# One tails product for two batches, loads reordered behind a DMA transpose, and query/key tails placed by GpSimd, in a fused attention and MLP-Mixer kernel

## The chip, the cores and the metric

The kernel runs on one core of a Trainium2 chip. Its time is the device time of one execution in microseconds (us), the median of several runs; lower is better. The core's engines are TensorE (PE in the profile, with its weight loads as PEld), VectorE (DVE), ScalarE (ACT), GpSimd (POOL) and SyncE (SP, which issues most of the DMAs). Each engine works through its own queue in order.

## The reference

```
q, k, v: [8, 8, 576, 64] float32          # batch, heads, sequence, head size
scores = q @ k^T / 8
  heads 0-3: only keys with 0 <= i - j < 32
  heads 4-7: only keys with 0 <= i - j < 128 and (i - j) % 4 == 0
x = softmax(scores) @ v                    # [8, 576, 512], heads side by side
h = relu(x^T @ w_tok1) @ w_tok2            # over the sequence: 576 -> 256 -> 576
u = x + h^T
out = u + relu(u @ w_ch1) @ w_ch2          # over the channels: 512 -> 1536 -> 512
```

## The kernel before

All matrix work is in float16 with float32 sums. The sequence of 576 is split into a main part of 512 (4 blocks of 128) and a tail of 64. The eight batches go through a software pipeline. Stage `b` of the program is the channel part of batch `b` (`gen_main(b)`): twelve products `gp` of 128 channels x 512 positions (L645), each followed by a relu into `gta` on ACT or DVE (L648); the tails product `gt` (L636); and then the second channel product `yp` (L664, in two halves for each of four blocks), to which DVE adds `u` (L674) before the result goes out. An odd batch has one more block, s = 4 (L684), that does the tails of two batches at once: the tails of the even batch lie in rows 0 to 63 of `u16t`, those of the odd one in rows 64 to 127, and their hidden values in columns 512 to 575 and 576 to 639 of `gta`.

The tails product is made batch by batch: `gp_tails` runs after channel blocks 5 and 8, each time for six channel blocks of 64 columns in one PSUM bank, four matmuls (one for each 128 channels of u) for each block: 24 matmuls of 64 columns.

Between the pieces of `gen_main(b)` come steps of other batches, which `interleave` places by a planner's clock: each piece of the main generator and each step has a cost in us, a step is emitted as soon as the clock has reached its due time, and what is left when the main generator ends is emitted at once. In a stage b from 2 on these steps are, with their due times:

- for batch b+1: the attention's value products (`values`), the token part (`emit_h1`, `emit_u`) and the turning of u (`uT_dma`, `uT_place`). For batches from 3 on, u is turned by a transposing DMA on SP's queue (`utt` for the tails, L570; `utm` for the main part, L572), and `uT_place` has ACT put two of the four blocks into natural order (`utd`, L582). For batches 0 to 2, `emit_uT` turns u by TensorE transposes and copies.
- for batch b+2: casts of q, k and v to float16 on GpSimd (`cast_steps`), transposing DMAs of q and k on SP (`dma_steps`, L349), placement of the turned q and k (`place_steps`), and the scores (`score_steps`). `plain` (pairs 0 and 1: three GpSimd copies each, L371 and L373), `tails` (L367, L368) and `dil` and `dil_k` (L377, L382) write the places that the score matmuls read. A pair's scores are three steps: `sc` for each of its two heads (L406) and `sm` for the parts at the end of the sequence, which reads the tails. ACT's exp follows, and for batches from 2 on GpSimd multiplies by the masks (L113).
- for batch b+3: fourteen load DMAs of q, k and v on SP's queue (`load_steps`).

Stages 0 and 1 have due times of their own. In stage 0 the scores of batch 1 and the first two pairs of batch 2 are made, in stage 1 the other two pairs of batch 2 and all of batch 3, the first batch whose q and k come by DMA.

Of the kernel before, what the change touches and what calls it, by code (L numbers as in the profile page):

```python
# [16 lines left out]
S = 576  # L17
# [52 lines left out]
def kernel(  # L70
# [16 lines left out]
    def fixed(name, shape, dtype=FP16):  # L87
        return sb.tile(shape, dtype, tag=name, bufs=1, name=name)
# [10 lines left out]
    def copy(eng, out, in_):  # L99
        if eng is nc.scalar:  # L100
            nc.scalar.copy(out=out, in_=in_)  # L101
        else:
            eng.tensor_copy(out=out, in_=in_)  # L103
# [48 lines left out]
    w4 = [w4a[:, i] for i in range(NMB)]  # L152
    idle = fixed("idle", [128, 512])
    uTm = [fixed(f"utm{i}", [128, 4, 4, 128]) for i in range(2)]
    uTt = [fixed(f"utt{i}", [128, 4, 128]) for i in range(2)]
    uTd = fixed("utd", [128, 2, 512])

    def emit_fixed():
# [202 lines left out]
    def place_steps(b):  # L361

        halves = [slice(0, 64), slice(64, 128)]

        def tails():
            for h in range(2):
                nc.vector.tensor_copy(out=qza[halves[h], :, h, 512:S], in_=tta[halves[h], :, 0:64])  # L367
            nc.vector.tensor_copy(out=kta[:, :, 512:S], in_=tta[:, :, 64:128])  # L368

        def plain(hp):  # L370
            nc.gpsimd.tensor_copy(out=natural(kt[hp][:, 0:512]), in_=kra[:, hp].rearrange("p r m -> p m r"))  # L371
            for h in range(2):
                nc.gpsimd.tensor_copy(out=natural(qz[hp][halves[h], h, 0:512]),  # L373
                                      in_=qta[halves[h], hp].rearrange("p r m -> p m r"))

        def dil(h):
            nc.vector.tensor_copy(out=qza[halves[h], 2:4, h, 0:512],  # L377
                                  in_=qta[halves[h], 2:4].rearrange("p a r m -> p a (r m)"))

        def dil_k():  # L380
            for hp in (2, 3):
                nc.vector.tensor_copy(out=natural(kt[hp][:, 384:512]),  # L382
                                      in_=kra[:, hp, :, 96:128].rearrange("p r m -> p m r"))

        return ([lambda hp=hp: plain(hp) for hp in range(2)],
                [tails] + [lambda h=h: dil(h) for h in range(2)] + [dil_k])

    def first_tails():

# [151 lines left out]
    def emit_uT(b, cb):  # L541
        odd = b % 2
        p = bank("fl" if b or cb % 2 == 0 else "main", 3, f"tpu_{b}_{cb}", FP16)
        tl = u16t[b // 2][:, cb]
        t = sb.tile([128, S], FP16, tag="ut", bufs=5, name=f"uT_{b}_{cb}")
        eng = nc.scalar if cb == 2 or (b and cb == 3) else nc.vector
        if cb < 2:
            m0, t0, c0 = (128, 0, 64) if odd else (0, 512, 0)
            for s in range(4):
                nc.tensor.transpose(out=p[:, m0 + 128 * s:m0 + 128 * s + 128],  # L550
                                    in_=u16(b, s)[:, cb], identity=ident)
            nc.tensor.transpose(out=p[:, t0:t0 + 128], in_=tl, identity=ident)
            copy(eng, t, p[:, c0:c0 + S])
        else:
            grid = p[:, 0:4 * RS].rearrange("p (r i) -> p r i", i=RS)
            m0, t0, c0 = (32, 0, 16) if odd else (0, 128, 0)
            for s in range(4):
                nc.tensor.transpose(out=grid[:, s, m0:m0 + 128], in_=u16(b, s)[:, cb], identity=ident)
            nc.tensor.transpose(out=grid[:, :, t0:t0 + 32], in_=tl, identity=perm)
            copy(eng, natural(t), grid[:, :, c0:c0 + MR].rearrange("p r m -> p m r"))  # L560
        uT[(b, cb)] = (t[:, 64:S], t[:, 0:64]) if odd else (t[:, 0:512], t[:, 512:S])


    def turned(b):
        return b >= 3
# [1 line left out]
    def uT_dma(b, tail):  # L567
        i = b % 2
        if tail:
            nc.sync.dma_start_transpose(out=uTt[i], in_=u16t[b // 2].rearrange("p x c -> p (x c)"))  # L570
        else:
            nc.sync.dma_start_transpose(out=uTm[i].rearrange("p x s t -> p (x s) t"),  # L572
                                        in_=u16w[b].rearrange("p x s c -> p (x s c)"))

    def uT_place(b, cb):
        i = b % 2
        tail = uTt[i][:, cb, 64 * i:64 * i + 64]
        if cb < 2:
            uT[(b, cb)] = (uTm[i][:, cb].rearrange("p s t -> p (s t)"), tail)
        else:  # L580
            uT[(b, cb)] = (uTd[:, cb - 2], tail)
            nc.scalar.copy(out=natural(uTd[:, cb - 2]), in_=uTm[i][:, cb].rearrange("p r m -> p m r"))  # L582
# [23 lines left out]
    def mix_steps(b, t_h1, t_h1b, t_u, t_uT, du=1.0):  # L606
        h1 = [sb.tile([128, DM], FP16, tag="h1", bufs=4, name=f"h1_{b}_{jb}") for jb in range(2)]
        steps = []
        for half, at in ((0, t_h1), (1, t_h1b)):
            for jb in range(2):  # L610
                steps.append((at + 0.9 * jb, 0.55, lambda jb=jb, half=half: emit_h1(b, jb, half, h1[jb])))
        for i, s in enumerate((4, 0, 1, 2, 3)):
            steps.append((t_u + du * i, 0.44, lambda s=s: emit_u(b, s, h1)))
        if turned(b):
            for t, tail in ((2.0, True), (6.0, False)):
                steps.append((t_u + t * du, 0.0, lambda tail=tail: uT_dma(b, tail)))
            for i, cb in enumerate(CBS):
                steps.append((t_uT + 0.5 * i, 0.0, lambda cb=cb: uT_place(b, cb)))
        else:
            for i, cb in enumerate(CBS):  # L620
                steps.append((t_uT + 0.9 * i, 0.28, lambda cb=cb: emit_uT(b, cb)))
        return steps

    def gen_main(b):
        odd = b % 2
        order = CBS if b else range(4)
        m0, t0 = (640, 576) if odd else (0, 512)

        def w3_block(cb, mb):
            return w3[cb][:, 512 * (mb // 4) + mb % 4:512 * (mb // 4) + 512:4]  # L630

        def gp_tails(half):
            p = bank("main", 3, f"gt_{b}_{half}")
            for i in range(6):
                for cb in order:
                    nc.tensor.matmul(  # L636
                        out=p[:, 64 * i:64 * i + 64], lhsT=w3_block(cb, 6 * half + i), rhs=uT[(b, cb)][1],
                        start=(cb == order[0]), stop=(cb == order[-1]))
            relu(nc.scalar if half else nc.vector, gta[:, 6 * half:6 * half + 6, t0:t0 + 64],
                 p[:, 0:384].rearrange("p (i t) -> p i t", t=64))  # L640

        for mb in range(NMB):
            p = bank("main", 3, f"gp_{b}_{mb}")
            for i, cb in enumerate(order):
                nc.tensor.matmul(out=p, lhsT=w3_block(cb, mb), rhs=uT[(b, cb)][0], start=(i == 0), stop=(i == 3))  # L645
                if i == 1:
                    yield 0.43
            relu(nc.vector if mb % (2 if b == 0 else 4) == 1 else nc.scalar, gta[:, mb, m0:m0 + 512], p)  # L648
            yield 0.43
            if mb in (5, 8):  # L650
                gp_tails(int(mb == 8))
                yield 0.7
        last = b == B - 1
        for s in ((4, 0, 1, 2, 3) if odd else (0, 1, 2, 3)):
            p = bank("main", 3, f"yp_{b}_{s}")
# [105 lines left out]
    for jb in range(2):  # L761
        nc.gpsimd.tensor_copy(
            out=w2p[jb], in_=w2[jb][:, 0:512].rearrange("p (m r) -> p r m", r=4))
    for i in range(2):
        nc.gpsimd.memset(u16t[i][64:128], 0.0)

    warm(8)
    ts = [st[2] for st in score_steps(0, 0.0, 1.0)]
# [109 lines left out]
    for b in range(B):  # L878
# [15 lines left out]
        elif b == 1:  # L894
            late = score_steps(2, -4.3, 2.4, (0.0, 0.7, 1.6))
            va = value_steps(2, 4.2, 1.0)
            steps += late[10:] + va[:4] + [(9.6 + (0.0, 0.8, 2.8, 3.6)[i], c, f) for i, (_, c, f) in enumerate(va[4:])]
            steps += mix_steps(2, 10.8, 14.6, 17.2, 22.2)
            steps += score_steps(3, 22.2, 2.8) + at(9.0, 0.6, cast_steps(3))
            steps += at(6.0, 0.0, [lambda: load_v(3)]) + at(20.0, 0.9, load_steps(4))  # L900
            steps += at(15.0, 0.7, dma_steps(3)) + at(20.6, 0.4, place_steps(3)[0])
            steps += [(t, 0.0, f) for t, f in zip((21.6, 27.0, 27.8, 28.6), place_steps(3)[1])]
        else:
            if b + 1 < B:
                steps += value_steps(b + 1, 0.4, 0.95) + mix_steps(b + 1, 5.4, 9.0, 11.4, 29.2)
            if b + 2 < B:
                steps += at(2.0, 0.6, cast_steps(b + 2)) + score_steps(b + 2, 16.2, 2.7)
                steps += at(8.5, 0.7, dma_steps(b + 2)) + at(13.0, 0.4, place_steps(b + 2)[0])
                steps += [(t, 0.0, f) for t, f in zip((15.5, 19.2, 20.0, 20.8), place_steps(b + 2)[1])]
            if b + 3 < B:  # L910
                steps += at(13.0, 0.9, load_steps(b + 3))
        interleave(gen_main(b), steps)


# [28 lines left out]
```

## Time and profile before

| what | us |
|---|---|
| median of 3 runs | 298.76 (298.59 to 299.44) |
| time of the profiled execution | 298.87 |
| its span, first to last instruction | 297.1 |
| PE busy | 283.5 (95%) |
| POOL busy | 181.6 (61%) |
| DVE busy | 155.6 (52%) |
| ACT busy | 132.1 (44%) |

The granted TensorE clock is 1.000. In the trace a line of a timeline gives the start in us, the duration, engine, source line, operation, output and inputs, shape and count, and in brackets the idle time before it with what ended it. A matmul's duration is its whole way through the array; matmuls follow each other much closer, so distances between starts are what counts. A row of the windows view gives for each engine the busy time in that stretch.

Stages begin at about 28.9 us (0), 70.7 (1), 107.9 (2), 140.1 (3), 174.1 (4) and 205.4 (5).

### The profile page before, as it was taken

The page shows a single profiled execution, that of the slowest core. Times are in us where ns is not written, and L with a number is a line of the kernel's source. Part 1 is how long each engine was busy: PE and PEld are TensorE (multiplying, and loading weights), DVE is VectorE, ACT ScalarE, POOL GpSimd, SP SyncE. Part 2 cuts the span into 40 slices and gives each one's busy share as a digit, 9 for nine tenths or more (in the row PEclk, how much of TensorE's full clock was granted, in tenths as well). Part 3 has the DMA queues.
Part 4 walks back from the last instruction along what each step waited for, and adds up shares of the span by engine and source line. Part 5 has one row for each costly group of instructions (what it writes and reads, how often), then busy time and mean ns, then how long its engine had stood idle before and what let it go on. Part 6 is the DMA issues. An engine that isn't in the chain of part 4 may idle for free.

```text
span 297.1 us, 7477 instructions
## 1 busy us (share of the span) xinstructions
PE 283.5 (95%) x3012; PEld 221.4 (75%) x3012; DVE 155.6 (52%) x328; ACT 132.1 (44%) x258; POOL 181.6 (61%) x245
## 2 busy tenths in 40 slices
PE   5698999999999999999999999999999999999994
PEld 2596579986767987688676977697777977796594
DVE  5776338656837966632745155723843265423022
ACT  2763326456652634347444544356345624323400
POOL 7992056428998899839992999459992920000000
PEclk9999999999999999999999999999999999999999
DMA  7999999953999699799679988499955220421023
GB/s 219 269 217 181 211 315 232 330 156 92 327 209 171 188 266 222 160 255 287 170 111 261 240 244 159 104 280 241 189 78 105 77 71 2 86 83 63 2 73 105
DMA packets 104562, 52.36 MB, mean 176 GB/s; under 512 B 72880, under 2 KB 103472, under 8 KB 104528
## 3 DMA queue, kind: packets, MB, share of 16 engines
q1 hardware_dynamic: 100288, 46.81, 65.6%
q0 software_dynamic: 2640, 3.91, 7.4%
q10 hardware_dynamic: 1600, 1.18, 1.3%
q8 instruction: 23, 0.38, 0.5%
q14 instruction: 11, 0.09, 0.1%
HBM read 37.04 MB, written 9.44 MB: 156 GB/s over the span
## 4 chain that ended last, share of the span: by engine, by line
PE 89%; DVE 4%; ACT 2%; DMA 2%; issue 1%; ACTq 0%; POOLq 0%
PE yp L664 27%; PE gp L645 27%; PE sc L406 5%; PE h1p L512 4%; PE gt L636 4%; PE up L524 4%; PE yp L684 4%; DMA const<-consts 2%; PE sm L406 2%; ACT utd L582 1%; PE av L482 1%; PE h1p L510 1%; PE av L493 1%; PE up L535 1%; PE sc L404 1%
## 5 line engine op out<-in xcount | busy, mean ns | idle before, releaser
L664 PE MATMUL yp<-w,gt 128*128 128x256 f16 x756 | 93.2, 273 | 0.7 <-DVE gt L109 0.7
L664 PEld LDWEIGHTS <-gt 128*128 128x128 f16 x768 | 76.5, 106 | 5.5 <-issue 0.9
L107 ACT ACTIVATE gt<-gp 128x512 f16<-128x512 f32 x69 | 41.2, 597 | 71.4 <-PE gp L645 71.1
L645 PEld LDWEIGHTS <-w 128*128 128x128 f16 x384 | 39.2, 114 | 22.7 <-issue 2.1
L113 POOL TENSOR_TENSOR attp<-attp,const 128x1280 f16<-128x1280 f16 (+1 forms) x24 | 36.4, 1543 | 30.2 <-ACT attp L435 30.0
L674 DVE TENSOR_TENSOR o<-yp,u 128x512 f32<-128x512 f32 x31 | 21.3, 690 | 57.6 <-PE yp L664 55.6
L645 PE MATMUL gp<-utd,w 128*128 128x512 f16 x120 | 45.6, 380 | 0.6 <-ACT utd L582 0.4
L645 PE MATMUL gp<-utm,w 128*128 128x512 f16 x120 | 45.5, 379 | 0.0
L645 PE MATMUL gp<-uT,w 128*128 128x512 f16 x144 | 37.3, 379 | 0.2 <-ACT uT L101 0.2
L113 POOL TENSOR_TENSOR attd<-attd,const 128x1024 f16<-128x1024 f16 (+1 forms) x24 | 32.8, 1399 | 0.0
L113 DVE TENSOR_TENSOR xn<-av,rec 128x320 f16<-128x320 f32 x64 | 31.5, 491 | 2.2
L109 DVE TENSOR_SCALAR gt<-gp 128x512 f16<-128x512 f32 x27 | 18.6, 688 | 17.3 <-PE gp L645 16.4
L406 PEld LDWEIGHTS <-kt 128*128 128x128 f16 x272 | 22.4, 101 | 4.1 <-DVE kt L315 1.7
L426 ACT ACTIVATE attp<-sc 128x480 f16<-128x480 f32 x32 | 17.7, 571 | 13.0 <-PE sc L406 12.3
L373 POOL COPY qz<-qt 64x512 f16<-64x512 f16 x20 | 21.5, 1077 | 0.6
L530 DVE TENSOR_TENSOR u<-up,xn 128x512 f16<-128x512 f32 x26 | 17.4, 689 | 8.3 <-PE up L524 8.1
L103 POOL CAST c_q<-l_q 128x512 f16<-128x512 f32 x31 | 19.2, 622 | 3.5 <-DMA l_q<-in_q_dram 3.5
L103 POOL CAST c_k<-l_k 128x512 f16<-128x512 f32 x29 | 17.8, 616 | 5.0 <-DMA l_k<-in_k_dram 4.1
L455 ACT ACTIVATE attd<-sc 128x512 f16<-128x512 f32 x32 | 18.7, 597 | 4.8 <-PE sc L406 4.2
L107 ACT ACTIVATE h<-h1p 128x256 f16<-128x256 f32 x28 | 10.7, 383 | 21.6 <-PE h1p L512 21.6
L406 PE MATMUL sc<-qz,kt 128*128 128x160 f16 (+1 forms) x144 | 18.1, 228 | 1.3 <-DVE kt L315 1.3
L501 DVE RECIPROCAL rec<-av 128x5 f32<-128x5 f32 x64 | 12.2, 190 | 13.6 <-PE av L488 7.0
(139 smaller groups left out, 487.1 us busy)
## 6 DMA issues: line engine op xcount, KB each, us to landing
out_dram<-o SPq DMA_DIRECT2D x72, 128.0 KB, 3.1
l_q<-in_q_dram SPq DMA_DIRECT2D x15, 512.0 KB, 6.3
l_k<-in_k_dram SPq DMA_DIRECT2D x14, 512.0 KB, 5.7
l_vn<-in_v_dram SPq DMA_DIRECT2D x32, 128.0 KB, 6.3
l_vd<-in_v_dram SPq DMA_DIRECT2D x16, 256.0 KB, 4.1
w<-in_moe_w_ch_dram POOLq DMA_DIRECT2D x6, 512.0 KB, 7.6
lt<-in_q_dram SPq DMA_DIRECT2D x8, 128.0 KB, 3.8
l_vt<-in_v_dram SPq DMA_DIRECT2D x8, 128.0 KB, 4.8
```

Of the source, the lines that this page charges most:

```text
L103: eng.tensor_copy(out=out, in_=in_)
L107: nc.scalar.activation(out=out, in_=in_, func=AF.Relu)
L109: eng.tensor_scalar_max(out=out, in0=in_, scalar1=0.0)
L113: eng.tensor_tensor(out=out, in0=x, in1=y, op=ALU.mult)
L373: nc.gpsimd.tensor_copy(out=natural(qz[hp][halves[h], h, 0:512]), in_=qta[halves[h], hp].rearrange("p r m -> p m r"))
L406: nc.tensor.matmul(out=out, lhsT=lhsT, rhs=qz[hp][:, h, queries], start=hide is None, stop=True)
L426: nc.scalar.activation(out=blocks[:, h, 0:3, 0:BLK], in_=p[:, 0:3 * BLK].rearrange("p (b c) -> p b c", c=BLK), func=AF.Exp, scale=0.125)
L455: nc.scalar.activation(out=a[:, h, 0:DTL], in_=p, func=AF.Exp, scale=0.125)
L530: nc.vector.tensor_tensor(out=u16(b, s), in0=blocks4(p), in1=blocks4(xn[b][:, s]), op=ALU.add)
L645: nc.tensor.matmul(out=p, lhsT=w3_block(cb, mb), rhs=uT[(b, cb)][0], start=(i == 0), stop=(i == 3))
L664: nc.tensor.matmul(out=p[:, c], lhsT=gta[:, mb, a0:m0 + 512:4] if half else gta[:, mb, a0:a0 + 128], rhs=w4[mb][:, c], start=(mb == 0), st ...
L674: nc.vector.tensor_tensor(out=blocks4(o32), in0=blocks4(p), in1=u16(b, s), op=ALU.add)
```

## The change

- The tails product is made once for two batches, in the odd batch: three groups (after channel blocks 3, 6 and 9), each of four channel blocks of 128 columns, 16 matmuls. An even batch has none. The even batch's tails need no turning of their own: `emit_uT` leaves them out in batches 0 and 2, and the transposing DMA of the tails is issued for odd batches only, into one buffer. The two memsets of `u16t` go.
- The copies of `tails()` go from DVE to GpSimd and come third behind the two `plain` steps.
- The relu of channel block 9 goes from DVE to ACT (batches from 1 on).
- In stages from 2 on, `load_steps` falls due at 17.6 instead of 13.0, which is behind the due time of u's transposing DMA.
- Scores fall due from 15.0 (even stages) or 17.4 (odd ones) in steps of 2.6, instead of from 16.2 in steps of 2.7; `dil`, `dil_k` and `uT_place` move too.

```diff
-    uTt = [fixed(f"utt{i}", [128, 4, 128]) for i in range(2)]
+    uTt = fixed("utt", [128, 4, 128])
...
         def tails():
             for h in range(2):
-                nc.vector.tensor_copy(out=qza[halves[h], :, h, 512:S], in_=tta[halves[h], :, 0:64])
-            nc.vector.tensor_copy(out=kta[:, :, 512:S], in_=tta[:, :, 64:128])
+                nc.gpsimd.tensor_copy(out=qza[halves[h], :, h, 512:S], in_=tta[halves[h], :, 0:64])
+            nc.gpsimd.tensor_copy(out=kta[:, :, 512:S], in_=tta[:, :, 64:128])
...
-        return ([lambda hp=hp: plain(hp) for hp in range(2)],
-                [tails] + [lambda h=h: dil(h) for h in range(2)] + [dil_k])
+        return ([lambda hp=hp: plain(hp) for hp in range(2)] + [tails],
+                [lambda h=h: dil(h) for h in range(2)] + [dil_k])
...
     def emit_uT(b, cb):
-        t = sb.tile([128, S], FP16, tag="ut", bufs=5, name=f"uT_{b}_{cb}")
+        t = sb.tile([128, 640 if odd else 512], FP16, tag=f"ut{odd}", bufs=4, name=f"uT_{b}_{cb}")
...
-            nc.tensor.transpose(out=p[:, t0:t0 + 128], in_=tl, identity=ident)
-            copy(eng, t, p[:, c0:c0 + S])
+            if odd:
+                nc.tensor.transpose(out=p[:, 0:128], in_=u16t[b // 2][:, cb], identity=ident)
+            copy(eng, t, p[:, 0:512 + m0])
...
-            for t, tail in ((2.0, True), (6.0, False)):
+            for t, tail in ((2.0, True), (6.0, False))[1 - b % 2:]:
...
-        m0, t0 = (640, 576) if odd else (0, 512)
+        m0 = 640 * odd
...
-        def gp_tails(half):
-            p = bank("main", 3, f"gt_{b}_{half}")
-            for i in range(6):
+        def gp_tails(g):
+            p = bank("main", 3, f"gt_{b}_{g}")
+            for i in range(4):
                 for cb in order:
                     nc.tensor.matmul(
-                        out=p[:, 64 * i:64 * i + 64], lhsT=w3_block(cb, 6 * half + i), rhs=uT[(b, cb)][1],
+                        out=p[:, 128 * i:128 * i + 128], lhsT=w3_block(cb, 4 * g + i), rhs=uT[(b, cb)][1],
                         start=(cb == order[0]), stop=(cb == order[-1]))
-            relu(nc.scalar if half else nc.vector, gta[:, 6 * half:6 * half + 6, t0:t0 + 64],
-                 p[:, 0:384].rearrange("p (i t) -> p i t", t=64))
+            relu(nc.scalar if g else nc.vector, gta[:, 4 * g:4 * g + 4, 512:640],
+                 p.rearrange("p (i t) -> p i t", t=128))
...
-            relu(nc.vector if mb % (2 if b == 0 else 4) == 1 else nc.scalar, gta[:, mb, m0:m0 + 512], p)
+            relu(nc.vector if (mb % 2 == 1 if b == 0 else mb in (1, 5)) else nc.scalar, gta[:, mb, m0:m0 + 512], p)
             yield 0.43
-            if mb in (5, 8):
-                gp_tails(int(mb == 8))
-                yield 0.7
+            if odd and mb in (3, 6, 9):
+                gp_tails(mb // 3 - 1)
+                yield 0.9
...
-    for i in range(2):
-        nc.gpsimd.memset(u16t[i][64:128], 0.0)
...
-            steps += [(t, 0.0, f) for t, f in zip((21.6, 27.0, 27.8, 28.6), place_steps(3)[1])]
+            steps += [(t, 0.0, f) for t, f in zip((27.0, 27.8, 28.6), place_steps(3)[1])]
         else:
+            late = 2.4 * (b % 2)
             if b + 1 < B:
-                steps += value_steps(b + 1, 0.4, 0.95) + mix_steps(b + 1, 5.4, 9.0, 11.4, 29.2)
+                steps += value_steps(b + 1, 0.4, 0.95) + mix_steps(b + 1, 5.4, 9.0, 11.4, 27.6 + late)
             if b + 2 < B:
-                steps += at(2.0, 0.6, cast_steps(b + 2)) + score_steps(b + 2, 16.2, 2.7)
+                steps += at(2.0, 0.6, cast_steps(b + 2)) + score_steps(b + 2, 15.0 + late, 2.6)
                 steps += at(8.5, 0.7, dma_steps(b + 2)) + at(13.0, 0.4, place_steps(b + 2)[0])
-                steps += [(t, 0.0, f) for t, f in zip((15.5, 19.2, 20.0, 20.8), place_steps(b + 2)[1])]
+                steps += [(t, 0.0, f) for t, f in zip((19.0 + late, 19.8 + late, 20.6 + late), place_steps(b + 2)[1])]
             if b + 3 < B:
-                steps += at(13.0, 0.9, load_steps(b + 3))
+                steps += at(17.6, 0.9, load_steps(b + 3))
```

More of the change, by code (lines that the diff above doesn't have):

```diff
@@ L543, in emit_uT @@
         p = bank("fl" if b or cb % 2 == 0 else "main", 3, f"tpu_{b}_{cb}", FP16)
-        tl = u16t[b // 2][:, cb]
-        t = sb.tile([128, S], FP16, tag="ut", bufs=5, name=f"uT_{b}_{cb}")
+        t = sb.tile([128, 640 if odd else 512], FP16, tag=f"ut{odd}", bufs=4, name=f"uT_{b}_{cb}")
         eng = nc.scalar if cb == 2 or (b and cb == 3) else nc.vector
+        m0 = 128 * odd
         if cb < 2:
-            m0, t0, c0 = (128, 0, 64) if odd else (0, 512, 0)
             for s in range(4):
@@ L551, in emit_uT @@
                                     in_=u16(b, s)[:, cb], identity=ident)
-            nc.tensor.transpose(out=p[:, t0:t0 + 128], in_=tl, identity=ident)
-            copy(eng, t, p[:, c0:c0 + S])
+            if odd:
+                nc.tensor.transpose(out=p[:, 0:128], in_=u16t[b // 2][:, cb], identity=ident)
+            copy(eng, t, p[:, 0:512 + m0])
         else:
             grid = p[:, 0:4 * RS].rearrange("p (r i) -> p r i", i=RS)
-            m0, t0, c0 = (32, 0, 16) if odd else (0, 128, 0)
+            m0 = 32 * odd
             for s in range(4):
                 nc.tensor.transpose(out=grid[:, s, m0:m0 + 128], in_=u16(b, s)[:, cb], identity=ident)
-            nc.tensor.transpose(out=grid[:, :, t0:t0 + 32], in_=tl, identity=perm)
-            copy(eng, natural(t), grid[:, :, c0:c0 + MR].rearrange("p r m -> p m r"))
-        uT[(b, cb)] = (t[:, 64:S], t[:, 0:64]) if odd else (t[:, 0:512], t[:, 512:S])
+            if odd:
+                nc.tensor.transpose(out=grid[:, :, 0:32], in_=u16t[b // 2][:, cb], identity=perm)
+            copy(eng, natural(t), grid[:, :, 0:128 + m0].rearrange("p r m -> p m r"))
+        uT[(b, cb)] = (t[:, 128:640], t[:, 0:128]) if odd else (t, None)
     def turned(b):
@@ L569, in uT_dma @@
         if tail:
-            nc.sync.dma_start_transpose(out=uTt[i], in_=u16t[b // 2].rearrange("p x c -> p (x c)"))
+            nc.sync.dma_start_transpose(out=uTt, in_=u16t[b // 2].rearrange("p x c -> p (x c)"))
         else:
@@ L576, in uT_place @@
         i = b % 2
-        tail = uTt[i][:, cb, 64 * i:64 * i + 64]
+        tail = uTt[:, cb]
         if cb < 2:
```

## The prediction

> **What bounds the kernel.** I read the page's busy shares and the chain that ended last, then TensorE's waits, then the order of the work at the places where the change moves something.
>
> ```profile
> span 297.1 us, 7477 instructions
> PE 283.5 (95%) x3012; PEld 221.4 (75%) x3012; DVE 155.6 (52%) x328; ACT 132.1 (44%) x258; POOL 181.6 (61%) x245
> PE 89%; DVE 4%; ACT 2%; DMA 2%; issue 1%; ACTq 0%; POOLq 0%
> PE yp L664 <- DVE gt L109: 0.7, 1, 0.7
> 71.40:99.10 27.70, 27.65 (x310) 20.47 (x309) 19.48 (x42) 13.12 (x26) 25.75 (x36) 1.00 0.94 208
> ```
>
> TensorE is the bound: 95% busy at the full clock, 89% of the chain, and its longest wait after the first 30 us is 0.7 us. So a matmul taken out of a stage is worth its spacing, if nothing else then ends last. But the last row has a second engine almost as full: from 71.4 to 99.1 us GpSimd is busy 25.75 of 27.70 us. Work given to GpSimd there, and TensorE made earlier there, is what I look at hardest.
>
> **The tails' product.** It is 24 matmuls of 64 columns, twice for every batch; after the change 16 of 128 columns, three times for each odd batch.
>
> ```profile
> 182.19 0.95 PE L636 MATMUL gt<-utt,w 128*128 128x64 f16 x24
> 182.98 0.38 PE L645 MATMUL gp<-utd,w 128*128 128x512 f16 x1
> 198.69 0.39 PE L406 MATMUL sc<-qz,kr 128*128 128x128 f16 x4
> 198.91 0.82 PE L664 MATMUL yp<-w,gt 128*128 128x256 f16 x6
> L636 PEld LDWEIGHTS <-w x384: 112/118/123, 34.2 to 277.4; 128*128 128x128 f16 x192
> ```
>
> From start to start, 24 of 64 columns take 182.98 - 182.19 = 0.79 us, 33 ns each; 4 of 128 columns take 0.22 us, 55 ns each. A group of 16 will be 0.88 us. An even stage loses 2 x 0.79 = 1.58 us, an odd stage goes from 1.58 to 2.64 (+1.06); over four pairs 384 x 33 ns = 12.7 us become 192 x 55 ns = 10.6 us, -2.1 us. The same strided weight loads (118 ns each, side by side) feed a matmul each 33 ns today, so 55 ns should be safe. The Trainium skill, "TensorE: Matmul & The Clock Gate", section "Back-to-back issue gap", speaks against the change: it gives about 81 ns for a weight load and a matmul of 128 columns in a real kernel; by it the product would take 192 x 81 ns = 15.6 us, 2.9 more than today, an estimate from that page. This trace does not agree, its pairs of 128 columns run at 55 ns.
>
> Batches 0 and 2 also lose 4 transposes each, 55 ns apiece by the same row: 0.22 us in stage 1, and as much ahead of stage 0. The relus shift: an even stage's ACT has 10 of 512 instead of 9 and one of 384, an odd stage's 12; DVE loses one in each; TensorE gives them 0.86 us apiece, and ACT's relu takes 0.60, so nothing.
>
> **Stage 0.** 1.58 us of product goes, but its end is a tail of h1, u, scores and uT without main work between, where ACT is dense.
>
> ```profile
> 60.00:71.40 11.40, 10.54 (x116) 9.04 (x114) 6.24 (x12) 8.41 (x19) 5.24 (x8) 1.00 0.43 120
> 61.83 0.38 ACT L107 ACTIVATE h<-h1p 128x256 f16<-128x256 f32 x1 [2.84 <-PE h1p L512]
> 71.45 0.59 PE L645 MATMUL gp<-uT,w 128*128 128x512 f16 x2 [0.17 <-ACT uT L101]
> ```
>
> ACT does its 8.41 us from 61.83 to 71.4, so that stretch can shrink by about 1.2 us at most. By the planner's due times the main generator, 1.4 units shorter, runs out before u, and two half blocks of yp (0.66 us each) that cover waits now come ahead of them. uT of batch 1 is copied 640 wide instead of 576, some 0.07 us on ACT at that end; its buffers and the single uTt are free long before. I take 1.2 us for stage 0 with the transposes, bounds 0.3 and 1.8.
>
> **Stage 1: the tails of q and k on GpSimd.** They become the third GpSimd step behind both plain placements; today DVE places them. TensorE's first reader is sm of batch 3.
>
> ```profile
> 67.61 2.98 POOL L113 TENSOR_TENSOR attp<-attp,const 128x1280 f16<-128x1280 f16 x2 [6.16 <-ACT attp L435]
> 67.61:91.05 23.44, 23.18 (x33) 1.00 0.92 204
> 91.42 1.07 POOL L371 COPY kt<-kr 128x512 f16<-128x512 f16 x1 [0.62 <-DMA kr<-c_k]
> 95.70 2.23 POOL L373 COPY qz<-qt 64x512 f16<-64x512 f16 x2
> 99.08 6.25 POOL L113 TENSOR_TENSOR attp<-attp,const 128x1280 f16<-128x1280 f16 x4 [1.15 <-ACT attp L435]
> 70.68 0.59 PE L645 MATMUL gp<-uT,w 128*128 128x512 f16 x2
> 96.52 0.82 PE L664 MATMUL yp<-w,gt 128*128 128x256 f16 x6
> 97.18 0.37 PE L406 MATMUL sc<-qz,kt 128*128 128x160 f16 x3
> 98.04 0.36 PE L406 MATMUL sm<-qz,kt 128*128 128x160 f16 x4
> 107.88 0.59 PE L645 MATMUL gp<-uT,w 128*128 128x512 f16 x2
> L103 POOL CAST vv<-l_vn 128x256 f16<-128x256 f32 x32 | 11.7, 409 | 0.0
> L373 POOL COPY qz<-qt 64x512 f16<-64x512 f16 x20 | 21.5, 1077 | 0.6
> ```
>
> GpSimd runs without a gap from its mask at 67.61 to 91.05, then, 0.6 us held by a transposing DMA, to the end of the plain placements at 97.93. That chain hangs on one exp at the end of stage 0, which I expect 0.6 us earlier (0 to 1.2), so the plain placements end at 97.3. The three tail copies have 256 elements per partition: 0.41 us each by the cast of 256, 0.54 by half the copy of 512; nearer in layout is the cast, so 3 x 0.41 = 1.2 us (bounds 1.1 and 1.6): the tails stand at 98.6 with the release.
>
> TensorE reaches sm today 98.04 - 70.68 = 27.36 us into the stage. By the order of emission it then has done one group of tails more and four transposes less (+1.06 - 0.22) and two half blocks of yp less (97.18 - 96.52 = 0.66 each): 26.9 us. The stage starts at 69.5, so it arrives at 96.4 and **waits 2.2 us** (0.5 to 3.5). What follows sm takes 107.88 - 98.04 = 9.84 us plus the two half blocks, 11.15: stage 2 starts at 109.8 instead of 107.88, **+1.9 us**; without the wait it would be -0.4. Behind the copies on GpSimd only this batch's masks wait; they need sm themselves.
>
> **Stages 2 to 5.** Here GpSimd has room: the copies fall into its idle time.
>
> ```profile
> 195.26 0.36 PE L406 MATMUL sm<-qz,kt 128*128 128x160 f16 x4
> 187.14 2.24 POOL L373 COPY qz<-qt 64x512 f16<-64x512 f16 x2
> 196.30 6.16 POOL L113 TENSOR_TENSOR attp<-attp,const 128x1280 f16<-128x1280 f16 x4 [6.93 <-ACT attp L435]
> 124.70 1.29 DVE L367 COPY qz<-tt 64x256 f16<-64x256 f16 x2
> 126.14 0.68 DVE L109 TENSOR_SCALAR gt<-gp 128x512 f16<-128x512 f32 x1
> ```
>
> In stage 4 the plain placements end at 189.38 and sm starts at 195.26, with 1.6 us less before it after the change: 4.3 us left for 1.2 us of copies. In stage 2 DVE's tail copies stand ahead of the relu at 126.14 that TensorE waited 0.7 us for; the copies leave DVE and mb 9's relu goes to ACT: -0.7 us.
>
> The scores' due times fall by 1.2 in even stages and rise by 1.2 in odd ones, as the main part does; in even stages the last sm still has two half blocks of yp behind it, as now, so the boundary gains nothing from the scores. But DVE's dil copies now come behind o of block 0 there, next to the masks.
>
> ```profile
> 192.08 0.86 DVE L377 COPY qz<-qt 64x1024 f16<-64x1024 f16 x2
> 195.46 0.69 DVE L674 TENSOR_TENSOR o<-yp,u 128x512 f32<-128x512 f32 x1 [2.52 <-PE yp L664]
> 98.85 3.17 DVE L377 COPY qz<-qt 64x1024 f16<-64x1024 f16 x2
> L113 POOL TENSOR_TENSOR attp<-attp,const 128x1280 f16<-128x1280 f16 x12 | 31.7, 2643 | 30.2 <-ACT attp L435 30.0
> ```
>
> Two such copies take 0.86 us alone and 3.17 us beside the mask at 99.08. In an even stage sm will start 19.65 us in, o's sum 0.2 later, so the dil copies at 20.5; the mask follows sm by 1.04 (196.30 - 195.26), at 20.7. The first copy gets in, the second waits for the 2.64 us mask until 23.5 and is done at 23.9 to 24.0; its reader, the second head of pair 2, comes at 23.95. I take 0.2 us in stages 2 and 4 (0 to 3.1). That the loser waits out the whole instruction is what the Trainium skill says ("SBUF — State Buffer", "Who interferes with whom"); the 3.17 us agree.
>
> **Loads behind the u transpose.**
>
> ```profile
> 119.74 0.67 SPq L197 DMA_DIRECT2D lt<-in_q_dram  x1
> 124.81 5.73 SPq L572 DMA_TRANSPOSE utm<-u  x1
> 138.50 0.45 SPq L208 DMA_DIRECT2D l_vx<-in_v_dram  x1
> 142.48 0.61 POOL L103 CAST c_t<-lt 128x512 f16<-128x512 f32 x1
> 150.56 0.39 POOL L103 CAST vt<-l_vx 128x256 f16<-128x256 f32 x1
> 138.97 2.08 ACT L582 COPY utd<-utm 128x512 f16<-128x512 f16 x2
> ```
>
> Five loads go ahead of utm today; after, all 14 follow its 5.73 us on SP, from about 132 to 142. They are first read by the casts from 142.48 on, the last at 150.56: a few us of cover, and GpSimd's idle 5 to 7 us behind it. utm itself is read only at 138.97, so its earlier issue gains nothing; nor does one tail transpose less in stages 3 and 5. I take 0 (-0.3 to +1.0). The two memsets of u16t go from GpSimd's idle first stage: 0.
>
> **The sum,** against the profiled execution, 298.87 us (span 297.1 and 1.77 around it; the median of the runs is 298.76): +1.9 up to stage 2's start; stages 2, 4, 6 each -1.58; 3, 5, 7 each +1.06; -0.7 for DVE's relu; 2 x 0.2 for the dil copies. 1.9 - 4.74 + 3.18 - 0.7 + 0.4 = +0.04, which is 298.9, or **298.8 us** against the median.
>
> **Rivals.**
> (B) No wait at sm of batch 3: the GpSimd chain comes 2 us earlier than I count, or tracks TensorE. Against it: 23.18 busy of 23.44 us. Then the terms are -0.4 and -1.86: 298.87 - 2.3 = 296.6, and 296.2 without the dil copies' 0.4.
> (C) Slower: the mask gets ahead of the first dil copy in even stages. It decides at 0.2 us (20.5 against 20.7). Pair 2 then waits at least 0.7 us, and up to 3.1 if a second mask of 2.64 and its tail of 0.44 pass too. Twice that: 300 to 305.
> (D) The loads come so late that casts starve GpSimd past its 5 us of idle time; one us is 299.9.
> (E) The weight loads do not hide behind 128 columns: at 118 ns each, 22.7 us instead of 10.6, 311. With the page's 81 ns it would be 303.9. The rows of 33 and 55 ns leave it little.
>
> **Chances.** Forecast 0.50, spread 297.6 to 300 by the wait's bounds; B 0.23, C 0.12, D 0.10, E 0.02, else 0.03. About 0.3% (0.9 us) is what a measurement tells from no change. Faster: B and a fringe of the forecast, 0.29; slower: C, E, half of D and a fringe, 0.21; same 0.50. The range 296.0 to 300.8 takes in B and the lower part of C; the likeliest case's own is 297.6 to 300.
>
> **What would show it.** gt groups of 16 spaced 0.88 us, three in odd stages, none in even ones. In stage 1 a wait of TensorE's sm (L406) for a GpSimd copy at L367 or L368 of about 2 us, and stage 2 starting near 109.8. No wait for gt L109 in stage 2. L377 spread over a mask in stages 2 and 4. The prediction is wrong if sm does not wait, if the copies take 2 us or more, or if TensorE waits at casts' products.

## The result, and the profile after

The changed kernel takes 300.95 us (median of 9 runs, 299.55 to 302.86) against 298.59 us (9 runs, 297.72 to 299.44): a ratio of 1.0077, 95% interval 1.0051 to 1.0104. It is slower, where 298.8 us was forecast, and 0.15 us above the range of 296.0 to 300.8. The profiled execution took 301.18 us.

The page of the changed kernel (span, busy times, the chain that ended last), and then the rows of TensorE's waits that before did not have; their columns are total us, number of waits, the longest:

```profile
span 299.2 us, 7051 instructions
PE 282.9 (95%) x2812; PEld 219.2 (73%) x2812; DVE 156.6 (52%) x302; ACT 137.2 (46%) x265; POOL 187.8 (63%) x258
PE 78%; POOL 9%; DVE 5%; ACT 3%; DMA 2%; issue 2%; POOLq 0%; ACTq 0%
```
```profile
PE sm L406 <- POOL qz L367: 0.7, 2, 0.4
PE h1p L510 <- ACT h L107: 0.6, 2, 0.3
PE sm L406 <- POOL kt L368: 0.2, 1, 0.2
```

200 matmuls are gone, but PE's busy time fell only 0.6 us, and its share of the chain from 89% to 78%: GpSimd now has 9%. The wait for `gt` is gone. In its place stand waits of `sm` for the tail copies on GpSimd, and of `h1p`. Where they fall is seen in the windows by stage, changed kernel (the first number after the stretch is its length, then come busy time and instructions of PE, PEld, DVE, ACT and POOL, the granted clock, the DMA share and GB/s; a stage runs from its first `gp` matmul to the next stage's, the last one to its last matmul):

```profile
29.52:71.43 41.91, 39.54 (x431) 31.43 (x429) 23.52 (x48) 20.18 (x43) 17.13 (x29) 1.00 1.02 261
71.43:110.97 39.54, 38.39 (x408) 30.00 (x406) 20.64 (x43) 19.84 (x41) 38.08 (x48) 1.00 0.79 208
110.97:140.76 29.79, 29.59 (x288) 23.12 (x287) 18.73 (x32) 14.92 (x30) 26.58 (x35) 1.00 0.64 157
140.76:176.25 35.49, 35.07 (x346) 27.22 (x346) 17.63 (x33) 17.94 (x33) 30.21 (x36) 1.00 0.89 214
176.25:206.05 29.80, 29.60 (x288) 23.11 (x287) 18.74 (x32) 14.92 (x30) 25.31 (x34) 1.00 0.78 193
206.05:241.82 35.77, 35.20 (x346) 27.22 (x346) 17.48 (x33) 18.00 (x33) 30.49 (x36) 1.00 0.64 139
```

Stages 0 to 3 of before:

```profile
28.91:70.68 41.77, 40.30 (x479) 33.10 (x477) 23.87 (x49) 20.74 (x44) 17.36 (x30) 1.00 0.91 232
70.68:107.88 37.20, 37.03 (x412) 29.11 (x410) 27.00 (x47) 18.63 (x39) 35.25 (x43) 1.00 0.91 219
107.88:140.10 32.22, 31.36 (x336) 24.71 (x335) 16.47 (x37) 14.75 (x30) 26.67 (x33) 1.00 1.03 231
140.10:174.07 33.97, 33.83 (x347) 25.98 (x347) 16.10 (x37) 16.64 (x31) 28.54 (x33) 1.00 0.87 208
```

All stages of both kernels against the prediction's terms, in us:

| stage | before | after | difference | predicted |
|---|---|---|---|---|
| 0 | 41.77 | 41.91 | +0.14 | -1.2 |
| 1 | 37.20 | 39.54 | +2.34 | +3.1, of it 2.2 the wait |
| 2 | 32.22 | 29.79 | -2.43 | -2.08 |
| 3 | 33.97 | 35.49 | +1.52 | +1.06 |
| 4 | 31.37 | 29.80 | -1.57 | -1.38 |
| 5 | 33.97 | 35.77 | +1.80 | +1.06 |
| 6 | 28.64 | 27.05 | -1.59 | -1.58 |
| 7 | 24.92 | 26.00 | +1.08 | +1.06 |
| sum | 264.06 | 265.35 | +1.29 | +0.04 |

The rest of the 2.1 us between the spans lies outside the stages: stage 0 starts 0.61 us later, and 0.2 us more lies behind the last matmul. The start turned out to move by itself (last section), so about 1.3 us is the change's.

Three of these rows give the loss: stage 0 won nothing, stage 1 waits, and stages 3 and 5 cost more than their matmuls. The wait in stage 1, on GpSimd and on TensorE, changed kernel:

```profile
68.68 2.99 POOL L113 TENSOR_TENSOR attp<-attp,const 128x1280 f16<-128x1280 f16 x2 [6.73 <-PE up L524]
96.14 2.21 POOL L373 COPY qz<-qt 64x512 f16<-64x512 f16 x2
98.41 1.02 POOL L367 COPY qz<-tt 64x256 f16<-64x256 f16 x2
99.50 0.40 POOL L368 COPY kt<-tt 128x256 f16<-128x256 f16 x1
```
```profile
97.74 0.82 PE L664 MATMUL yp<-w,gt 128*128 128x256 f16 x6
98.95 0.23 PE L406 MATMUL sm<-qz,kt 128*128 128x160 f16 x1 [0.39 <-POOL qz L367]
99.49 0.23 PE L406 MATMUL sm<-qz,kt 128*128 128x160 f16 x1 [0.31 <-POOL qz L367]
99.95 0.23 PE L406 MATMUL sm<-qz,kt 128*128 128x64 f16 x2 [0.23 <-POOL kt L368]
```

Each `sm` matmul starts just after one tail copy lands (copies end at about 98.9, 99.4 and 99.90). The brackets count PE's idle time only from a matmul's modelled end. From the starts more is missing: six `yp` half matmuls take 6 x 0.11 = 0.66 us, so the first `sm` could have started at 98.40; it starts 0.55 late, and the next two come 0.54 and 0.46 after their forerunners instead of about 0.07 (160 columns, scaled from the 0.216 us between `gp` matmuls of 512). In all 0.55 + 0.47 + 0.39 = 1.4 us.

In stages 3 and 5 the first tails group and the token part collide. TensorE in stage 3, changed kernel:

```profile
145.80 1.05 PE L636 MATMUL gt<-utt,w 128*128 128x128 f16 x16
146.69 0.28 PE L493 MATMUL av<-vv,attd 128*128 128x65 f16 x4
146.87 0.27 PE L510 MATMUL h1p<-xn,w1t 128*128 128x256 f16 x1
147.42 0.28 PE L493 MATMUL av<-vv,attd 128*128 128x65 f16 x4
148.06 0.27 PE L510 MATMUL h1p<-xn,w1t 128*128 128x256 f16 x1 [0.29 <-ACT h L107]
```

The group of 16 takes 146.69 - 145.80 = 0.89 us (0.88 was predicted). By then the planner's clock has passed the due times of several steps, and they are emitted without a `gp` block between: value products, `h1p`, value products, `h1p`. The second `h1p` would follow at 147.60; it comes 0.45 us later, released by ACT's relu of the first.

### The profile page after: what moved, and what is told of

It is laid out like the page before. It is cut to its first block, busy times and chain, and to the rows that moved or that the text cites. A ratio compares the mean times of both kernels' runs of the same rounds, so it can differ in the third digit from the quotient of the medians.

```text
span 299.2 us, 7051 instructions
## 1 busy us (share of the span) xinstructions
PE 282.9 (95%) x2812; PEld 219.2 (73%) x2812; DVE 156.6 (52%) x302; ACT 137.2 (46%) x265; POOL 187.8 (63%) x258
## 4 chain that ended last, share of the span: by engine, by line
PE 78%; POOL 9%; DVE 5%; ACT 3%; DMA 2%; issue 2%; POOLq 0%; ACTq 0%
PE yp L664 25%; PE gp L645 24%; PE sc L406 4%; PE h1p L512 4%; PE up L524 3%; PE gt L636 3%; PE yp L684 3%; POOL vv L103 2%; DMA const<-consts 2%; POOL attd L113 2%; POOL qz L373 1%; ACT utd L582 1%; PE sm L406 1%; PE h1p L510 1%; PE av L482 1%
## 5 line engine op out<-in xcount | busy, mean ns | idle before, releaser
L664 PE MATMUL yp<-w,gt 128*128 128x256 f16 x756 | 92.0, 273 | 0.0
L107 ACT ACTIVATE gt<-gp 128x512 f16<-128x512 f32 x76 | 45.4, 597 | 71.0 <-PE gp L645 70.7
L645 PEld LDWEIGHTS <-w 128*128 128x128 f16 x384 | 40.1, 114 | 24.4 <-issue 2.1
L113 POOL TENSOR_TENSOR attp<-attp,const 128x1280 f16<-128x1280 f16 (+1 forms) x24 | 37.2, 1574 | 16.4 <-ACT attp L435 9.6
L645 PE MATMUL gp<-uT,w 128*128 128x512 f16 x144 | 36.3, 379 | 0.2 <-ACT uT L101 0.2
L530 DVE TENSOR_TENSOR u<-up,xn 128x512 f16<-128x512 f32 x26 | 18.0, 691 | 7.9 <-PE up L524 7.9
L109 DVE TENSOR_SCALAR gt<-gp 128x512 f16<-128x512 f32 x20 | 13.8, 688 | 11.7 <-PE gp L645 11.3
```

Of the source, the lines that this page charges most:

```text
L107: nc.scalar.activation(out=out, in_=in_, func=AF.Relu)
L109: eng.tensor_scalar_max(out=out, in0=in_, scalar1=0.0)
L113: eng.tensor_tensor(out=out, in0=x, in1=y, op=ALU.mult)
L530: nc.vector.tensor_tensor(out=u16(b, s), in0=blocks4(p), in1=blocks4(xn[b][:, s]), op=ALU.add)
L664: nc.tensor.matmul(out=p[:, c], lhsT=gta[:, mb, a0:m0 + 512:4] if half else gta[:, mb, a0:a0 + 128], rhs=w4[mb][:, c], start=(mb == 0), st ...
```

## The experiments

Each edit is against the changed kernel unless it says otherwise. Stage lengths are read from each profiled execution as above; ratios are to the kernel before, timed beside it on the same chip, and can differ by some 0.2% from the quotient of two medians.

**Stage 1: the copies' engine.**

```diff
-                nc.gpsimd.tensor_copy(out=qza[halves[h], :, h, 512:S], in_=tta[halves[h], :, 0:64])
-            nc.gpsimd.tensor_copy(out=kta[:, :, 512:S], in_=tta[:, :, 64:128])
+                nc.vector.tensor_copy(out=qza[halves[h], :, h, 512:S], in_=tta[halves[h], :, 0:64])
+            nc.vector.tensor_copy(out=kta[:, :, 512:S], in_=tta[:, :, 64:128])
```

> The changed kernel with the copies of q's and k's tails put back from GpSimd to VectorE, in the same place of the program. Theory (the wait of sm of batch 3 for GpSimd is paid by the copies there): the three waits at sm in stage 1, 1.4 us in start-to-start distances, go, stage 1 is 38.1 us instead of 39.5, and the kernel is 1.4 us faster than the changed one, about 299.5. Rival (GpSimd's plain placements, or VectorE's copies held up by GpSimd, take the wait's place): stage 1 stays within 0.5 us of 39.5 and the time near 301.

298.82 us, ratio 1.0004 (0.9985 to 1.0023). Its window of stage 1:

```profile
69.65:107.76 38.11, 37.88 (x407) 30.00 (x405) 22.56 (x46) 19.84 (x41) 36.78 (x45) 1.00 0.90 236
```

38.11 us instead of 39.54: the copies on GpSimd cost 1.43 us, and only here; no other stage moved by more than 0.02. Is it the engine, or the place in its queue?

**Stage 1: the place in GpSimd's queue.**

```diff
-        return ([lambda hp=hp: plain(hp) for hp in range(2)] + [tails],
+        return ([lambda: plain(0), tails, lambda: plain(1)],
```

> The changed kernel with GpSimd's tail copies emitted between the two plain placements instead of behind them. Theory (sm of batch 3 waits for its place in GpSimd's queue, not for GpSimd as such): sm waits no more, but sc of pair 1, 0.85 us later, then waits some 0.7 us for the second plain placement: stage 1 about 38.9 us instead of 39.5, the time 0.7 us below the changed kernel's. Rival (the copies cost their 1.4 us wherever they stand): stage 1 stays at 39.4 to 39.6.

298.4 us, ratio 1.0002 (0.9978 to 1.0026). GpSimd, and the window of stage 1:

```profile
94.59 0.85 POOL L367 COPY qz<-tt 64x256 f16<-64x256 f16 x2
95.50 0.40 POOL L368 COPY kt<-tt 128x256 f16<-128x256 f16 x1
96.86 2.56 POOL L373 COPY qz<-qt 64x512 f16<-64x512 f16 x2
```
```profile
70.91:109.02 38.11, 37.89 (x408) 30.00 (x405) 21.12 (x43) 19.84 (x41) 37.73 (x48) 1.00 0.79 207
```

The same 38.11 us with the copies still on GpSimd. So the place is what cost; the tails stand at 95.9, 2 us ahead of `sm`. The new wait of 0.7 us that I expected for pair 1's placement, now behind the tails, did not come: that placement ends at 99.42, its reader starts at 99.60, and TensorE shows no wait there.

**Stage 0: the due times.** The main generator of stage 0 is 1.4 units shorter (two groups of 0.7), but the steps between kept their due times. All of them 1.4 sooner:

```diff
             steps += at(36.0, 0.0, [lambda: emit_loads_qk(3)])
+            steps = [(p - 1.4, c, f) for p, c, f in steps]
```

> The changed kernel with all due times of stage 0 taken 1.4 earlier, which is what the main generator lost there. Theory (stage 0 gained nothing because its steps kept their due times, so that the main work that covered their waits ran out early): stage 0 goes from 41.9 to 40.3 us, its waits from 4.5 back to about 2.9, and as GpSimd's masks of batch 2 move with it the wait in stage 1 stays: the kernel is 1.5 us faster than the changed one, about 299.4. Rival (ScalarE's and VectorE's own work at the end of stage 0 sets its end): stage 0 stays at 41.5 to 42 and the time near 301.

297.4 us, ratio 0.9971 (0.9953 to 0.9990). Stage 0 and 1:

```profile
27.67:67.77 40.10, 38.86 (x432) 31.53 (x430) 23.28 (x48) 20.44 (x43) 17.75 (x31) 1.00 1.03 251
67.77:106.88 39.11, 38.34 (x408) 29.98 (x406) 20.23 (x43) 19.83 (x41) 37.65 (x47) 1.00 0.96 245
```

Stage 0 falls by 1.81 us, from 41.91 to 40.10, with not an instruction less on any engine: the saving of 1.58 us was there and was eaten by waits. Counted by start distances (what a distance has above the usual one, where that is more than 0.05 us), TensorE waits 2.6 us in stage 0 of the kernel before, 4.3 in the changed kernel and 2.5 in this run; 1.4 of the 1.7 us that came with the change lie in the last 10 us of the stage. The waits stand where TensorE reaches a step whose input isn't there yet, for example these two in the changed kernel, which stage 0 of before does not have:

```profile
49.11 0.24 PE L406 MATMUL sc<-qz,kt 128*128 128x160 f16 x1 [0.30 <-DVE kt L315]
64.23 0.59 PE L535 MATMUL up<-h,w 128*128 128x512 f16 x2 [0.29 <-DVE h L109]
```

Both are gone in this run. Stage 1 falls too, by 0.43 us, which I had not expected: the first `sm` matmul starts 0.11 us late instead of 0.55, as GpSimd's chain has moved further forward than TensorE. But is the pull good in itself, or only as the counterpart of the shorter generator? The same line in the kernel before:

> The kernel before with every due time of stage 0 moved 1.4 forward and nothing else. Theory (stage 0 of the changed kernel lost its gain because the due times stood while the main generator had become 1.4 shorter): here the generator is as long as it was, so the old due times fit it; stage 0 stays at 41.8 us within 0.5, and the time within 0.6 us of before. Rival (the due times of stage 0 were late in any case, and the 1.8 us won by moving them has nothing to do with the product): stage 0 falls to about 40.0 to 40.5 us and the time by 1.3 to 1.8 us.

298.09 us, ratio 0.9999 (0.9980 to 1.0018):

```profile
27.82:69.34 41.52, 40.30 (x479) 33.05 (x477) 23.99 (x49) 20.96 (x44) 18.18 (x32) 1.00 1.00 257
```

With the old generator the same pull brings 0.25 us, not 1.8. From 41.77 us, 1.58 of product and 0.25 of this would make 39.94; the 40.10 above, and 39.86 and 39.85 in the last two kernels below, whose stage 0 has the same code, lie around it. They also show that stage 0 differs by 0.25 us between traces of one code, so the 0.25 may be nothing. The due times fitted the work they were written for, and not the work that was left.

**The joint product by itself,** on the kernel before: `emit_uT` without even tails, one `uTt`, three groups of 16 in odd batches behind blocks 3, 6 and 9, no memsets; tail copies, relus, loads and all due times as before.

> The kernel before with the joint tails product alone (uT without the even batches' tails, three groups of 16 in odd stages, no memsets): tails of q and k on VectorE, loads ahead, all due times and relus as before. Theory: TensorE loses 1.95 us of matmuls and 0.2 to 0.4 of transposes, but gives back 1.5 in stage 0 (due times) and 1 to 1.3 us at the end of each of stages 2 and 4, where the last scores and uT_place now fall due as the main generator ends: about 299 to 301. Rival (the product's saving reaches the end): 296.5 to 297.

300.94 us, ratio 1.0071 (1.0044 to 1.0098): alone it costs as much as the whole change. Stage 0 is the changed kernel's, 41.91 us, and stage 1 has no wait, 38.11. Stages 2 and 4, ACT's copies at the end of stage 2, and the row of waits for them:

```profile
109.20:140.28 31.08, 29.60 (x289) 23.18 (x288) 15.60 (x36) 14.30 (x29) 25.17 (x32) 1.00 0.80 191
175.67:206.75 31.08, 29.60 (x289) 23.16 (x287) 15.60 (x36) 14.29 (x29) 22.83 (x29) 1.00 0.75 184
```
```profile
139.17 2.03 ACT L582 COPY utd<-utm 128x512 f16<-128x512 f16 x2
```
```profile
PE gp L645 <- ACT utd L582: 3.0, 2, 1.5
```

The stage's product ends 1.58 us sooner, its last scores and `uT_place` don't, and the next stage's first `gp` waits for `utd`. That is 31.08 - 29.79 = 1.29 us twice. In the changed kernel these waits are small (0.4 us, two of them, as before); it has the scores and `uT_place` earlier in even stages. Which of the two earns how much of the 1.29 us is not separated here. In stage 0 no due time was corrected. Stages 3 and 5 are 35.39 us each, both with the wait at `h1p`: it comes with the product alone.

**The first tails group.** Behind blocks 5, 8 and 10 instead of 3, 6 and 9:

```diff
-            if odd and mb in (3, 6, 9):
-                gp_tails(mb // 3 - 1)
+            if odd and mb in (5, 8, 10):
+                gp_tails((5, 8, 10).index(mb))
```

> The changed kernel with the three groups of the tails product behind channel blocks 5, 8 and 10 instead of 3, 6 and 9. Theory (the group behind block 3 takes main work away from between the first two h1 products, whose PSUM bank then is not free): the waits of 0.45 us at h1p in stages 3 and 5 go, those stages are 35.0 and 35.3 us instead of 35.5 and 35.8, 0.9 us in all. Rival (the wait only moves to another h1p or to av): 35.4 and 35.7 as now.

298.96 us, ratio 1.0014 (0.9996 to 1.0032). Stage 3, whole and in TensorE's rows (stage 5: 35.34 us):

```profile
139.28:174.33 35.05, 34.91 (x347) 27.13 (x347) 18.18 (x33) 17.88 (x33) 30.26 (x36) 1.00 0.91 217
```
```profile
145.35 0.27 PE L510 MATMUL h1p<-xn,w1t 128*128 128x256 f16 x1
146.08 0.27 PE L510 MATMUL h1p<-xn,w1t 128*128 128x256 f16 x1
```

0.44 us less in stage 3 and 0.43 in stage 5; `h1p` follows `h1p` by 0.73 us without a wait. Stage 5 keeps 0.3 us that stage 3 hasn't: a score matmul that starts at 230.69, 26.6 us into the stage, just after ACT's exp at L438 ends. The joint product by itself does not have it (35.39 us in both stages), so it comes with another part of the change; which one is open.

**The loads.** Due at 13.0 again, ahead of u's transposing DMA:

```diff
-                steps += at(17.6, 0.9, load_steps(b + 3))
+                steps += at(13.0, 0.9, load_steps(b + 3))
```

> The changed kernel with the loads due at 13.0 again, ahead of u's DMA transpose. Theory (the order of the loads is hidden both ways): within 0.3 us of the changed kernel, about 301, no wait of GpSimd's casts in either. Rival (late loads are what costs): 1 us or more faster, near 299.5. Second rival (the transposes come sooner and that helped): slower by 0.5 us or more.

299.78 us, ratio 1.0054 (1.0033 to 1.0075); every stage is within 0.02 us of the changed kernel's. The order of loads and transpose is worth nothing either way.

**The changed kernel once more,** without an edit, beside the runs above:

> The changed kernel itself once more, beside the kernel before, to weigh the time up to stage 0, which was 27.7 to 29.5 us in six traces whose code is nearly the same there. Theory (that part differs by chance, from the DMAs of the start): the stages from 0 on have the lengths of the first trace within 0.1 us each, 1.3 us more in all than the kernel before, and the time lies 1.3 to 2.3 us over the kernel before, near a ratio of 1.005. Rival (the changed kernel starts later by its code): stage 0 starts at 29.5 again and the ratio is 1.0077.

299.63 us, ratio 1.0052 (1.0027 to 1.0076). All stages are within 0.03 us of the first trace, and stage 0 starts at 27.74 instead of 29.52. So 1.5 rather than 2.4 us is nearer to what the change costs, and the stages' +1.29 agrees with it; the two ratios' intervals overlap.

**The three mends together:** tail copies on DVE, stage 0's due times 1.4 sooner, the groups behind blocks 5, 8 and 10.

> The changed kernel with three mendings at once: tail copies on VectorE, stage 0's due times 1.4 earlier, and the groups of the tails product behind blocks 5, 8 and 10. Theory (the three losses add and are separate): stage 0 about 40.1, stage 1 38.1, stages 3 and 5 0.45 us shorter each: 1.8 + 1.4 + 0.9 = 4.1 us below the changed kernel from stage 0 on, 2.8 below the kernel before, a ratio near 0.990. Rival (what is won in one place is waited out in the next): no better than with the due times alone, 0.997.

296.12 us, ratio 0.9913 (0.9883 to 0.9943), faster than both kernels. The stages sum to 261.00 us, 4.35 less than the changed kernel's; the single mends had won 1.81, 1.43 and 0.44 + 0.43, 4.11 in all. The other 0.24 is stage 0, 39.86 us instead of 40.10 with the same code.

**One wait more.** What is left at the starts of stages 3 and 5 is the wait for `utd` that before had too. So `uT_place` 1.6 sooner, on top of the three:

```diff
-                steps += value_steps(b + 1, 0.4, 0.95) + mix_steps(b + 1, 5.4, 9.0, 11.4, 27.6 + late)
+                steps += value_steps(b + 1, 0.4, 0.95) + mix_steps(b + 1, 5.4, 9.0, 11.4, 26.0 + late)
```

> The kernel with the three mends, and uT_place due at 26.0 instead of 27.6 in even stages (28.4 instead of 30.0 in odd ones). In the three mends' kernel ACT's two copies into utd run from 136.47 for 2.09 us, behind the last exp, and stages 3 and 5 begin with waits of 0.36 and 0.30 us for them. Theory (the place of uT_place in ACT's queue alone sets these waits): both waits go, stages 3 and 5 fall from 35.06 and 35.33 us by about 0.65 each, the time by 1.3 us. Rival (the last exps, which the copies now stand ahead of, are needed at once): a wait for an exp or a free bank of the scores appears at the end of stages 2 and 4, up to 2.1 us each, and the time is unchanged or up to 3 us longer.

294.37 us, ratio 0.9862 (0.9828 to 0.9895). ACT at the end of stage 2, and the windows of stages 2 and 3:

```profile
133.20 0.59 ACT L455 ACTIVATE attd<-sc 128x512 f16<-128x512 f32 x1
133.68 1.09 ACT L582 COPY utd<-utm 128x512 f16<-128x512 f16 x1
134.67 0.60 ACT L455 ACTIVATE attd<-sc 128x512 f16<-128x512 f32 x1
135.16 1.09 ACT L582 COPY utd<-utm 128x512 f16<-128x512 f16 x1
```
```profile
107.06:136.49 29.43, 29.43 (x288) 23.12 (x287) 20.15 (x34) 15.61 (x30) 24.93 (x31) 1.00 0.65 158
136.49:171.26 34.77, 34.77 (x348) 26.99 (x347) 18.71 (x36) 16.89 (x33) 29.38 (x34) 1.00 0.95 232
```

The copies slip between the exps and the wait is gone on both sides of the boundary: in both windows PE is busy from end to end. Stages 2 to 5 lose 0.3 to 0.4 us each, 1.3 in all, where I had put 0.65 each on stages 3 and 5 alone: of the two waits at a boundary the first is counted in the stage before. The exps behind the copies were not needed at once.

## Why the prediction was wrong, point by point

**The product: right.** Groups of 0.89 us (0.88 predicted), none in even stages. Stages 4, 6 and 7, where nothing else hangs on it, changed by -1.57, -1.59 and +1.08 against the product's own -1.58, -1.58 and +1.06. 16 matmuls in 0.89 us are 56 ns apiece: the 81 ns of the Trainium skill, "TensorE: Matmul & The Clock Gate", "Back-to-back issue gap", do not hold for this loop, and rival E is out.

**Stage 0: the step that failed.** "I take 1.2 us for stage 0 with the transposes, bounds 0.3 and 1.8": it lost 0.14. I took ACT's density in the last 11 us as the limit and let all else follow the main generator. The limit was elsewhere: steps emitted by a clock that still ran to the old sum. I had noted that the generator now runs out sooner, and that two half blocks of `yp` no longer cover waits at the end; the end is where most of the new waits are. The mis-sized term is the price of the waits that this brings: some 0.4 us (1.58 down to 1.2) in the prediction, 1.7 us in the trace. With the due times moved the same instructions take 1.81 us less, while the same move in the old kernel brings 0.25. ACT's density, which I gave as the reason for 1.2 and not 1.58, was no limit either: the stage then lies 1.67 us below before, with ACT's work as it was.

**The wait in stage 1: mechanism right, size off.** "Waits 2.2 us" measured 1.4, because both sides came later than predicted. TensorE reached `sm` 26.97 us into the stage (26.9 predicted), but the stage began at 71.43 instead of 69.5, as stage 0 gave nothing: 2.0 us later. The tails stood at 99.90 instead of 98.6, 1.3 us later: GpSimd's chain began at 68.68 instead of 67.0, the copies took 1.49 us and not 1.2, and the 0.6 us for the transposing DMA, still in the sum, were gone. Stage 1 itself was 0.76 us shorter than the +3.1 said. Rival B (no wait) is out; the copies' place costs 1.43.

**Stages 3 and 5: a cost I did not list.** I priced the group and not the place where it was put. Behind block 3 it let token steps pile up: 0.45 us in each, 0.9 together. The other 0.3 us in stage 5 are not the group's, and their cause is open.

**Stage 2: right in size, its cause not shown.** TensorE's wait for DVE's relu is gone, 32.22 to 29.79. I put that down to the tail copies leaving DVE and the relu of block 9 going to ACT. But in the run of the joint product by itself, where both stayed on DVE, the wait is gone too, since the relu now comes ahead of the copies:

```profile
123.11 0.68 DVE L109 TENSOR_SCALAR gt<-gp 128x512 f16<-128x512 f32 x1
126.14 0.46 DVE L367 COPY qz<-tt 64x256 f16<-64x256 f16 x2
```

So the product alone is enough for it; no run shows that the two moves were needed. The dil copies do collide with the mask, as predicted for the second of them; DVE and GpSimd in stage 2 of the changed kernel:

```profile
131.38 3.17 DVE L377 COPY qz<-qt 64x1024 f16<-64x1024 f16 x2
131.54 6.32 POOL L113 TENSOR_TENSOR attp<-attp,const 128x1280 f16<-128x1280 f16 x4 [2.86 <-ACT attp L435]
```

3.17 us for two copies of 0.43 each, the second held behind the first mask; it ends at 134.55, and the reader's matmul starts at 134.91. The cover of 0.2 us that I charged was not needed: cost 0 in stages 2 and 4. Rival C is out: its condition was that the mask gets ahead of the first dil copy, and that copy starts 0.16 us before the mask (0.2 predicted).

**Loads: right at 0.** Rival D is out.

**The sum.** Against the terms, in order: stage 0 +1.34, stage 1 -0.76, stage 2 -0.35, stages 3 and 5 +0.46 and +0.74, stage 4 -0.19, rest 0.01: +1.25, which is the stages' +1.29 instead of +0.04. The start and the end added 0.8. The range went to 300.8 by way of rival C, and so named a loss of that size for a reason that did not happen. Whether the time falls just above that bound (300.95) or inside the range (299.63, the second measurement) hangs, as far as the traces show, on where stage 0 starts (29.52 and 27.74 us), which is luck; that stage 0 gave nothing is not.

## What to carry to other kernels

When work is taken out of a schedule that places other work by a clock, everything placed behind it should move by as much, or the saving can turn into waits at the first steps that now come due too late: here 1.8 us in stage 0, and 1.29 us at each boundary where only half of the change was made. Ask for each stage which due times were written for the old sum, and price a new block of work by what it pushes together as well as by its own length. For copies handed to an engine with a full queue, look at the place in the queue before the engine: here second instead of third was the whole 1.43 us.

## What the runs showed of the hardware that I had not expected

The same few instructions near the start can go two ways. DVE's cast of `l_vt` and GpSimd's cast of `l_vd` start within 20 ns of each other. The changed kernel, and the run with the tails between:

```profile
15.75 1.48 DVE L103 CAST vv<-l_vt 64x512 f16<-64x512 f32 x1
15.77 1.18 POOL L103 CAST vv<-l_vd 128x512 f16<-128x512 f32 x2
```
```profile
15.88 0.41 DVE L103 CAST vv<-l_vt 64x512 f16<-64x512 f32 x1
15.90 1.43 POOL L103 CAST vv<-l_vd 128x512 f16<-128x512 f32 x2
```

In the first DVE's cast takes 1.48 us and ends 0.28 us behind GpSimd's pair, in the second it takes 0.41 us and GpSimd's pair is the longer one by 0.25. The Trainium skill, "SBUF — State Buffer", "Who interferes with whom", says that when DVE works in a two-port mode, the one of DVE and GpSimd that issues first gets the ports they share for the whole instruction, and the other is blocked. The 1.48 us against 0.41 agree with such a blocking, here by both casts of the pair; no run shows in which mode the cast works, and the order can't be read from the starts on record, since DVE's stands 20 ns ahead in both.

Stage 0 began between 27.67 and 29.84 us in twelve traces whose code up to there is nearly the same. The two in which DVE's cast took 1.48 us are the latest (29.52 and 29.84); in the six that began before 28.1 us DVE's cast starts 0.75 us or more ahead of GpSimd's pair, and what brings it there sooner is not shown. Two single traces that differ by a microsecond or two should be compared from the first stage on, not by their spans.
